# Reading both heads' scores out before the transposes, one copy moved to ScalarE, partial sums added later

## The chip, the cores and the metric

The kernel runs on one core of one Trainium2 chip. The metric is the time of one execution on the device, in microseconds (us); lower is better. The core has five engines with a queue each, which meet only through semaphores: TensorE (PE in the profile, its weight loads PEld), VectorE (DVE), ScalarE (ACT), GpSimd (POOL) and SyncE (SP, which here only issues DMAs). TensorE multiplies out of SBUF into PSUM, which has eight banks of 512 fp32 numbers in each of 128 partitions.

## The reference

Three parts follow one another: attention with a computed bias, a max-of-three layer, and an ELU layer.

```python
# q, k, v: 4 batches, 8 heads, 576 rows, 64 wide
scores = q @ k.T / sqrt(64) + bias          # bias from a small network of |i - j| and i
attn   = softmax(scores)                    # over 576 keys
x      = (attn @ v) as [2304, 512]
h      = max(x @ w1, x @ w2, x @ w3)        # 512 -> 768
x      = h @ w_out                          # 768 -> 512
out    = ELU(x @ w_in) @ w_out2             # 512 -> 2048 -> 512
```

All inputs are fp32, the weights of the later layers are given as 64-bit numbers that the kernel turns into fp32 itself.

## The kernel before

A first stage (to about 66 us) computes the bias and stores it to DRAM. The attention follows (to about 404 us), then the two layers, in which TensorE is busy nearly all of the time.

The attention works through 16 pairs of heads (n), and five blocks of query rows for each (c = 0 to 4): 80 steps, s = 5n + c. Blocks 0 to 3 are 128 rows of both heads; block 4 is the last 64 rows of both heads, packed into one tile of 128 partitions, so it has one read-out instead of two. I call five steps a group and name a step by the block whose scores it computes (step 0 to step 4).

What belongs to one block, in its order:
- `unit_qk` (L222, PE): scores of one head into one of two PSUM tiles, PB[0] and PB[1] (pb in the rows), two banks each.
- `scores` (L230, DVE): reads a head's scores out of PB, adds the bias and finds the row's extreme. I call the two of a step h0 and h1.
- `expo` (L235, ACT): the exponential, with its row sum.
- `recip` (L240, L241, DVE) and `diag` (L249, POOL): the reciprocal of the row sums, as a diagonal matrix.
- `trans` (L252, PE): turns the exponentials into the two PSUM tiles TQ (tq) and scales them with that diagonal, 32 products that the trace lists as 64 matmuls. The first 512 of the 576 keys fit there.
- `tails` (L252, PE): the last 64 keys of each head, turned into unused columns of PB[0], 4 products (8 matmuls). They lie in the same two banks as head 0's scores.
- `evac_tails` (L77, DVE) copies the tails out of PB[0]; `evac` (L75 on ACT or L77 on DVE) copies TQ[0] and TQ[1] out. EVD lists the blocks whose TQ[1] goes to DVE.
- `pv` (L319, L323, L327, PE): products with v into two PSUM tiles XO (xo), after the blocks 0 and 1, and after 2 to 4. When they are complete, `x_copy` (L341, ACT) takes XO[0], `x_sum` (L345, DVE) adds XO[1], `x_hi` and `x_lo` (POOL) split the sum into two parts for the next layer.
- `pump` (L420 to L430 and others): one piece of the decoding of a later layer's weights. Nearly all of them put one instruction on DVE, some one on ACT or POOL. One goes with each step past the sixth, except where c = 1.

The order is set by numbers. Every call is entered in a plan with a key, s plus an offset out of the table OFF; the plan is sorted by key and issued in that order, and each engine executes its own instructions strictly so. An offset above 1 or 2 means that the call is made one or two steps later: in step s, TensorE computes the scores of block s, turns the exponentials of block s - 2, and multiplies older blocks with v. Waits are derived from the order: a call that touches a PSUM bank which an earlier call of another engine touched waits for that call.

Of the kernel before, what the change touches and what calls it, by code (L numbers as in the profile page):

```python
# [31 lines left out]

OFF = {"qk0": 0.0, "qk1": 0.01, "t0": 0.30, "t1": 0.31, "pump": 0.32, "ns": 1.305, "dg": 1.306, "tr": 2.10, "tl": 2.20,
       "evt": 2.311, "ev0": 2.385, "ev1": 2.387, "ex0": 0.38, "ex1": 0.40}
PV_AT = {1: [(4.5, 0), (4.5, 1), (5.5, 2), (5.5, 3), (5.5, 4)],
         4: [(3.5, 0), (3.5, 1), (4.5, 2), (4.5, 3), (5.5, 4)]}
X_AT = {1: 5.6, 4: 5.6}
EVD = {0, 1, 2}  # L40

MOE_LD = 74.39
MOE_AT = [(79.60, 81.00), (80.60, 81.45), (82.00, None)]
# [10 lines left out]
def fused_kernel(ctx, tc, tkq, vv, lt, pk, wm1, wo1, win2, wo2, out):  # L54
# [16 lines left out]
    def hi_of(eng, dst, src):  # L71
        if eng == "p":
            nc.gpsimd.tensor_scalar(dst, src, 1.0, 1.0, op0=ALU.mult, op1=ALU.mult)
        elif eng == "a":
            nc.scalar.activation(dst, src, AF.Copy)  # L75
        else:
            nc.vector.tensor_copy(dst, src)  # L77
# [43 lines left out]
    with ExitStack() as pro:  # L121
# [18 lines left out]
        with tc.manual_schedule():  # L140
# [38 lines left out]
            for A in range(36):  # L179
# [15 lines left out]
                c, r = divmod(A, 8)  # L195
# [94 lines left out]
    def evac(s, g):  # L290
        n, c = steps[s]
        p = PT[n, c > 1][0]
        if c < 4:
            q0 = 128 * (c % 2) + 64 * g
            hi_of("v" if g and c in EVD else "a", p[:, :, q0:q0 + 64], TQ[g].rearrange("p (k q) -> p k q", k=8))
        else:
# [251 lines left out]
    def at(key, fn, *args):  # L548
        plan.append((key, len(plan), fn, args))

    for s, (n, c) in enumerate(steps):
        o = {nm: s + off for nm, off in OFF.items()}
        at(o["qk0"], unit_qk, s, 0)
        at(o["t0"], scores, s, 0)
        at(o["ex0"], expo, s, 0)
        if c < 4:
            at(o["qk1"], unit_qk, s, 1)
            at(o["t1"], scores, s, 1)
            at(o["ex1"], expo, s, 1)
        at(o["ns"], recip, s)  # L560
        at(o["dg"], diag, s)
        at(o["tr"], trans, s)
        at(o["tl"], tails, s)
        at(o["ev0"], evac, s, 0)
        at(o["ev1"], evac, s, 1)
        at(o["evt"], evac_tails, s)
        if c in (1, 4):
            for off, k in PV_AT[c]:
                at(s + off + 0.01 * k, pv, s, k)
            at(s + X_AT[c], x_copy, s)  # L570
            at(s + X_AT[c] + 0.25, x_sum, s)
            at(s + X_AT[c] + 0.5, x_hi, s)
            at(s + X_AT[c] + 0.75, x_lo, s)
        if s > 5 and c != 1:
            at(o["pump"], pump)
        if n % 4 == 3 and n < 15:
            at(s + 0.45, load_b, n // 4 + 1, c)
# [121 lines left out]
    def small(tag, bufs):  # L699
        return mp.tile([128, NB], F32, tag=tag, name=f"{tag}_t", bufs=bufs)  # L700
# [61 lines left out]
    with tc.manual_schedule():  # L762
        for n, u in enumerate(units + [None]):
# [6 lines left out]
            if n < 2:  # L770

                for i in range(2):
                    w = take_w(("wi", u[1], 3 * i))
                    v = take_w(("w3", pre[1], i)) if pre else None
                    for q, (b, d) in enumerate(((B11, B21), (B12, B22))):
# [3 lines left out]
                        c = small("c", 4)  # L779
# [121 lines left out]
```

## Time and profile before

| | |
|---|---|
| Runs | 1098.22, 1095.53, 1097.67 us; median 1097.67 |
| Profiled execution | 1097.02 us, of which the span of instructions is 1095.2 |
| PE | busy 989.3 us, 90% of the span |
| DVE | 708.7 us, 65% |
| ACT | 517.6 us, 47% |
| POOL | 339.3 us, 31% |
| Chain that ended last | PE 80%, DVE 16%, all others 4% |

The busy shares are means over stages with different limits. In the page's 40 slices PE is at 7 or 8 tenths in the attention and at 9 or more from the sixteenth slice on; DVE stands at 6 to 9 tenths in the attention. The 16% of the chain that run through DVE lie mostly in the attention.

### The profile page before, as it was taken

How to read it: one execution, taken by the hardware profiler on the slowest of the kernel's cores; microseconds unless marked ns; L12 is line 12 of the kernel's file. 1: busy time of each engine (PE TensorE's matmuls, PEld its weight loads, DVE VectorE, ACT ScalarE, POOL GpSimd, SP SyncE). 2: the span in 40 equal slices, each digit the busy share in tenths (PEclk: the TensorE clock that was granted, in tenths of full speed). 3: DMA queues.
4: the chain of work that ended last, by engine and by line, in shares of the span. 5: the costliest groups of instructions: out<-in, count | busy, mean ns of one | idle time of the engine just before them, and what ended most of it. 6: DMA issues, size and time to landing. Idle time of an engine off the chain costs nothing.

```text
span 1095.2 us, 28524 instructions
## 1 busy us (share of the span) xinstructions
PE 989.3 (90%) x11748; PEld 846.2 (77%) x11748; DVE 708.7 (65%) x1444; ACT 517.6 (47%) x1071; POOL 339.3 (31%) x419
## 2 busy tenths in 40 slices
PE   7967777777777679999999999999999999999998
PEld 3445555555455468999999999998999889988997
DVE  7946676667666665998878698174567436663333
ACT  8935555555555553333343334163445344444433
POOL 0002323223322233444345345122332323232212
PEclk9979999999999999999999999999999999999999
DMA  7731443343352213567798788325556655575553
GB/s 274 280 122 67 139 144 116 127 142 118 108 172 86 86 58 129 194 221 286 257 350 307 247 293 323 117 97 174 178 192 210 237 176 194 193 253 180 188 194 110
DMA packets 65905, 201.00 MB, mean 184 GB/s; under 512 B 7024, under 2 KB 14832, under 8 KB 65776
## 3 DMA queue, kind: packets, MB, share of 16 engines
q1 hardware_dynamic: 65776, 199.18, 53.0%
q8 instruction: 93, 1.52, 0.5%
q14 instruction: 36, 0.29, 0.1%
HBM read 150.78 MB, written 48.37 MB: 182 GB/s over the span
## 4 chain that ended last, share of the span: by engine, by line
PE 80%; DVE 16%; issue 2%; DMA 1%; ACT 0%; SPq 0%; POOL 0%; DVEq 0%; POOLq 0%; ACTq 0%
PE xo L696 16%; PE pb L740 12%; PE pb L526 11%; DVE e_t L230 9%; PE tq L252 7%; PE tq L740 6%; PE pb L222 5%; PE xo L526 5%; PE tq L526 5%; PE pb L620 3%; DVE p L77 3%; PE pb L183 2%; PE pbb L183 2%; PE xo L620 2%; PE tq L620 2%
## 5 line engine op out<-in xcount | busy, mean ns | idle before, releaser
L81 POOL TENSOR_TENSOR gl<-t_t,gh 128x384 fp32r<-128x384 f32 x96 | 108.8, 1144 | 286.0 <-ACT gh L75 286.0
L235 ACT ACTIVATE e_t<-e_t,st_t 128x576 f32<-128x576 f32 x144 | 111.1, 772 | 164.1 <-DVE st_t L240 155.2
L230 DVE CUSTOM_DVE_ANT_0 e_t<-pb,b_t 128x576 f32<-128x576 f32 x144 | 107.7, 748 | 88.3 <-PE pb L252 67.5
L222 PE MATMUL pb<-kq_t 64*64 64x288 f32 x1152 | 90.9, 425 | 74.0 <-DVE p L77 72.8
L249 POOL TENSOR_SCALAR dg_t<-ident,st_t 128x64 f32<-128x64 f32 x144 | 49.8, 359 | 264.3 <-DVE st_t L241 192.1
L222 PEld LDWEIGHTS pb<-kq_t 64*64 64x64 f32 x1152 | 36.5, 134 | 120.9 <-DVE p L77 105.8
L252 PEld LDWEIGHTS tq<-dg_t,e_t 64*64 64x64 f32 x4608 | 91.0, 139 | 41.0 <-DVE p L77 17.1
L740 PE MATMUL pb<-w_t,gh 128*128 128x512 f32 x384 | 119.3, 392 | 0.0
L526 PE MATMUL pb<-xh,w_t 128*128 128x384 f32 x448 | 116.9, 336 | 0.0
L252 PE MATMUL tq<-dg_t,e_t 64*64 64x64 f32 x4608 | 96.4, 225 | 18.5 <-DVE p L77 12.5
L696 PE MATMUL xo<-tt,w_t 128*128 128x384 f32 x528 | 107.4, 338 | 0.0
L696 PEld LDWEIGHTS xo<-tt,w_t 128*128 128x128 f32 x528 | 95.0, 188 | 7.5
L718 ACT ACTIVATE t_t<-c_t 128x384 f32<-128x384 f32 x96 | 50.0, 521 | 103.7 <-DVE c_t L709 95.5
L696 PE MATMUL xo<-xh,w_t 128*128 128x384 f32 x328 | 94.6, 335 | 0.0
L526 PEld LDWEIGHTS pb<-xh,w_t 128*128 128x128 f32 x448 | 81.2, 188 | 0.5 <-issue 0.4
L319 PE MATMUL xo<-p,tv_t 64*64 64x320 f32 (+1 forms) x1024 | 78.7, 408 | 0.9 <-issue 0.5
L740 PEld LDWEIGHTS pb<-w_t,gh 128*128 128x128 f32 x384 | 70.5, 188 | 6.6
L740 PE MATMUL pb<-w_t,gl 128*128 128x512 f32 x192 | 75.5, 393 | 0.0
L526 PE MATMUL pb<-xl,w_t 128*128 128x384 f32 x224 | 75.3, 336 | 0.0
L75 ACT ACTIVATE gh<-t_t 128x384 fp32r<-128x384 f32 x96 | 48.5, 519 | 33.4 <-DVE t_t L726 33.4
L696 PEld LDWEIGHTS xo<-xh,w_t 128*128 128x128 f32 x328 | 60.2, 188 | 3.0
L726 DVE SCALAR_TENSOR_TENSOR t_t<-t_t,c_t 128x384 f32<-128x384 f32 x96 | 59.0, 632 | 4.5 <-ACT t_t L719 4.1
(131 smaller groups left out, 2198.8 us busy)
## 6 DMA issues: line engine op xcount, KB each, us to landing
w_t<-scw_w SPq DMA_DIRECT2D x90, 512.0 KB, 4.4
w_t<-scw_wi SPq DMA_DIRECT2D x74, 512.0 KB, 3.6
kq_t<-tkq SPq DMA_DIRECT2D x16, 864.0 KB, 5.2
scw_wi<-sp SPq DMA_DIRECT2D x26, 512.0 KB, 4.7
scw_w<-sp SPq DMA_DIRECT2D x22, 512.0 KB, 5.3
raw<-wo SPq DMA_DIRECT2D x22, 512.0 KB, 3.8
scr<-o_t SPq DMA_DIRECT2D x36, 288.0 KB, 3.9
raw<-wm SPq DMA_DIRECT2D x18, 512.0 KB, 3.9
```

Source lines behind the costliest of these rows:

```text
L81: e.tensor_tensor(out=dst, in0=src, in1=hi.bitcast(F32), op=ALU.subtract)
L222: mm(PB[h][H64[g], 224 + 288 * r:512 + 288 * r], t[H64[r], 576 + 576 * a + q0:640 + 576 * a + q0], t[H64[r], 288 * a:288 * a + 288], start ...
L230: nc.vector.tensor_tensor_reduce(out=E[s][:, 576 * h:576 * h + 576], in0=PB[h][:, 224:800], in1=BT[n // 4, c, h], op0=ALU.add, op1=ALU.min ...
L235: nc.scalar.activation(e, e, AF.Exp, bias=st[:, h:h + 1], scale=-1.0, accum_out=st[:, 2 + h:3 + h])
L252: mm(dst, E[s][H64[g], k0:k0 + 64], DG[s][H64[g], h % nheads(s)], start=True, stop=True)
L319: mm(XO[g][H64[h], 0:w], v[H64[g], 128 * k + 64 * h:128 * k + 64 * h + 64], ps[0][H64[g], 4 * h + k, :], start=(k == 0), stop=(k == 3 and ...
L526: mm(ps[blk][:, 0:NB], wt[:, ks], xt[:, kk, t0:t0 + NB], start=(j == 0), stop=(j == 11))
L620: mm(ps[blk][:, 0:NB], WO[0][:, kk, wt, ms], xt[:, bs], start=(j == 0), stop=(j == 3 * NM1 - 1))
L696: mm(ps, w[wt][:, ks], b[xt][:, kk], start=(start and j == 0), stop=(stop and j == 5), skip_group_check=True)
L718: nc.scalar.activation(t, c, AF.Relu, scale=-1.0)
L726: pend.append([lambda: nc.vector.scalar_tensor_tensor(out=t, in0=t, scalar=-1.0, in1=c, op0=ALU.add, op1=ALU.max), last])
L740: mm(acc[t], g[:, ts], w[k], start=(f == 0 and i == 0 and j == 0), stop=(f == NU - 1 and i == 1 and j == 2))
```

## The change

Three entries of the tables and one offset change. `t0` and `t1` (h0 and h1) go from 0.30 and 0.31, behind `trans` and `tails`, to 0.02 and 0.03, ahead of them. `recip` and `diag` of the block before keep their place between the two read-outs. Block 1 leaves EVD, so the copy of its TQ[1] goes to ACT. `x_sum` goes from 0.25 to 0.427 behind `x_copy`, which is past the start of the next step, between `recip` and h1.

```diff
-OFF = {"qk0": 0.0, "qk1": 0.01, "t0": 0.30, "t1": 0.31, "pump": 0.32, "ns": 1.305, "dg": 1.306, "tr": 2.10, "tl": 2.20,
-       "evt": 2.311, "ev0": 2.385, "ev1": 2.387, "ex0": 0.38, "ex1": 0.40}
+OFF = {"qk0": 0.0, "qk1": 0.01, "t0": 0.02, "ns": 1.025, "dg": 1.026, "t1": 0.03, "tr": 2.10, "tl": 2.20, "evt": 2.311,
+       "pump": 0.32, "ev0": 2.385, "ev1": 2.387, "ex0": 0.38, "ex1": 0.40}
...
-EVD = {0, 1, 2}
+EVD = {0, 2}
...
-            at(s + X_AT[c] + 0.25, x_sum, s)
+            at(s + X_AT[c] + 0.427, x_sum, s)
```

On DVE, one whole step 3, before and then now; pb_99 is PB[0], pb_100 is PB[1], tq_860 is TQ[1], ISA is the read-out of scores or of its extreme, and the brackets name the engine whose semaphore is waited for.

```order
L230 ISA e_t,st_t<-pb_99,b_t 128x576 [waits PE_49]
L230 ISA st_t 128x1
L240 TENSOR_SCALAR st_t<-st_t 128x2 [waits Activation_49]
L241 RECIPROCAL st_t<-st_t 128x2 [waits DVE_49]
L230 ISA e_t,st_t<-pb_100,b_t 128x576
L230 ISA st_t 128x1
L77 COPY p_5274<-pb_99 128x128
L430 TENSOR_TENSOR t_w<-t_w,x_t 128x512
L77 COPY p_5273<-tq_860 128x8x64
```

```order
L230 ISA e_t,st_t<-pb_99,b_t 128x576 [waits PE_49]
L230 ISA st_t 128x1
L240 TENSOR_SCALAR st_t<-st_t 128x2 [waits Activation_49]
L241 RECIPROCAL st_t<-st_t 128x2 [waits DVE_49]
L230 ISA e_t,st_t<-pb_100,b_t 128x576 [waits PE_49]
L230 ISA st_t 128x1
L77 COPY p_5283<-pb_99 128x128 [waits PE_49]
L430 TENSOR_TENSOR t_w<-t_w,x_t 128x512
```

DVE's order is the same but for the copy of TQ[1], which is gone; but h1 and the copy of the tails, which before had nothing left to wait for once h0 had started, now have waits on PE of their own.

On PE, the end of the turning and the tails of one step, before and then now; xo_861 and xo_862 are XO[0] and XO[1].

```order
L252 MATMUL tq_859<-dg_t,e_t 64x64 x2
L252 MATMUL tq_860<-dg_t,e_t 64x64 x2
L252 MATMUL pb_99<-dg_t,e_t 64x64 x4
L319 MATMUL xo_861<-p_4252,tv_t 64x256 [waits DMAHW2_49,Activation_49]
L319 MATMUL xo_861<-p_4252,tv_t 64x256
L319 MATMUL xo_862<-p_4252,tv_t 64x256 [waits DVE_49]
```

```order
L252 MATMUL tq_859<-dg_t,e_t 64x64 x2
L252 MATMUL tq_860<-dg_t,e_t 64x64 x2
L252 MATMUL pb_99<-dg_t,e_t 64x64 [waits DVE_49]
L252 MATMUL pb_99<-dg_t,e_t 64x64 x3
L319 MATMUL xo_861<-p_4261,tv_t 64x256 [waits DMAHW2_49,Activation_49]
L319 MATMUL xo_861<-p_4261,tv_t 64x256
L319 MATMUL xo_862<-p_4261,tv_t 64x256 [waits DVE_49]
```

No matmul has moved; the first product of the tails has got a wait on DVE.

On DVE again, from the end of a step 4 into step 0, before and then now; L345 is `x_sum`.

```order
L77 COPY p_5410<-pb_99 128x128
L420 TENSOR_SCALAR x_t<-raw 128x512 [waits DMAHW4_49]
L77 COPY p_5409<-tq_860 128x8x64
L345 TENSOR_TENSOR xf<-xo_862,xf 128x320 [waits Activation_49]
L230 ISA e_t,st_t<-pb_99,b_t 128x576 [waits PE_49]
L230 ISA st_t 128x1
L240 TENSOR_SCALAR st_t<-st_t 128x1
L241 RECIPROCAL st_t<-st_t 128x1 [waits DVE_49]
L230 ISA e_t,st_t<-pb_100,b_t 128x576
```

```order
L77 COPY p_5418<-pb_99 128x128 [waits PE_49]
L420 TENSOR_SCALAR x_t<-raw 128x512 [waits DMAHW4_49]
L77 COPY p_5417<-tq_860 128x8x64
L230 ISA e_t,st_t<-pb_99,b_t 128x576 [waits PE_49]
L230 ISA st_t 128x1
L240 TENSOR_SCALAR st_t<-st_t 128x1 [waits Activation_49]
L241 RECIPROCAL st_t<-st_t 128x1 [waits DVE_49]
L345 TENSOR_TENSOR xf<-xo_862,xf 128x320 [waits Activation_49]
L230 ISA e_t,st_t<-pb_100,b_t 128x576 [waits PE_49]
```

`x_sum` has moved from ahead of h0 to between the reciprocal and h1.

## Rows read from the trace of the kernel before

**Rows 1.** Busy us by engine in two stretches, then clock, DMA share, GB/s.

```profile
66.00:78.00 12.00, 7.93 (x196) 6.03 (x188) 4.95 (x16) 4.21 (x10) 1.22 (x4) 0.50 0.07 10
90.00:400.00 310.00, 228.95 (x6724) 160.47 (x6720) 210.81 (x601) 169.04 (x407) 93.01 (x196) 0.99 0.35 118
```

**Rows 2.** Waits from 90 to 404 us: who for whom, us, times, longest.

```profile
ACT e_t L235 <- DVE st_t L240: 142.1, 72, 3.6
...
PE pb L222 <- DVE p L77: 65.5, 71, 1.1
DVE e_t L230 <- PE pb L252: 54.5, 58, 2.5
```

**Rows 3.** Chain of waits through a step 2 and beyond: start, us on it.

```profile
259.04 1.20 PE pb L222 x16
260.24 0.93 PE tq L252 x64
261.17 0.16 PE pb L252 x8
...
261.36 0.76 DVE e_t L230
...
262.40 0.65 DVE e_t L230
...
263.06 0.20 DVE p L77
263.27 1.14 DVE t_w L425
264.41 0.61 DVE p L77
```

**Rows 4.** Timeline of PE, starts of step 4, second and last group: start, us, instruction.

```profile
96.74 0.72 PE L222 MATMUL pb<-kq_t 64*64 64x288 f32 x8 [1.04 <-DVE p L77]
...
401.53 0.72 PE L222 MATMUL pb<-kq_t 64*64 64x288 f32 x8 [0.94 <-DVE p L77]
```

**Rows 5.** Timeline of PE: a step 4 begins, and a step 2.

```profile
268.35 0.72 PE L222 MATMUL pb<-kq_t 64*64 64x288 f32 x8 [0.94 <-DVE p L77]
268.88 0.29 PE L252 MATMUL tq<-dg_t,e_t 64*64 64x64 f32 x4
...
280.39 1.20 PE L222 MATMUL pb<-kq_t 64*64 64x288 f32 x16 [0.72 <-DVE p L77]
281.41 1.11 PE L252 MATMUL tq<-dg_t,e_t 64*64 64x64 f32 x64
282.34 0.30 PE L252 MATMUL pb<-dg_t,e_t 64*64 64x64 f32 x8
282.46 1.26 PE L319 MATMUL xo<-p,tv_t 64*64 64x320 f32 x16
```

**Rows 6.** Timeline of DVE in a step 1.

```profile
278.43 0.76 DVE L230 CUSTOM_DVE_ANT_0 e_t<-pb,b_t 128x576 f32<-128x576 f32 x1 [1.11 <-PE pb L252]
...
279.11 0.17 DVE L240 TENSOR_SCALAR st_t<-st_t 128x2 f32<-128x2 f32 x1
...
279.39 0.74 DVE L230 CUSTOM_DVE_ANT_0 e_t<-pb,b_t 128x576 f32<-128x576 f32 x1
...
280.06 0.28 DVE L77 COPY p<-pb 64x128 f32<-64x128 f32 x1
281.76 0.42 DVE L345 TENSOR_TENSOR xf<-xo,xf 128x256 f32<-128x256 f32 x1 [1.42 <-ACT xf L341]
```

**Rows 7.** Two decoding lines, 90 to 404 us: ns least/median/most.

```profile
L423 DVE TENSOR_SCALAR t_w<-raw x13: 410/1245/1517, 96.6 to 398.1; 128x512 int32<-128x512 int32 x13
...
L425 DVE SCALAR_TENSOR_TENSOR t_w<-raw,t_w x13: 680/691/1236, 100.2 to 401.4; 128x512 int32<-128x512 int32 x13
```

**Rows 8.** Timeline of ACT: two copies of TQ, then the second exponential.

```profile
276.30 1.07 ACT L75 ACTIVATE p<-tq 128x512 f32<-128x512 f32 x2
277.25 0.77 ACT L235 ACTIVATE e_t<-e_t,st_t 128x576 f32<-128x576 f32 x1
```

## The prediction

> **What bounds the kernel now.** I read the windows by stage first, then the waits, then the chain of waits through a few steps, and last the timelines of single engines for durations. In the attention from 90 to 400 us PE is busy 228.95 of 310 us and DVE 210.81, at a granted clock of 0.99 [rows 1]: neither is full, so the stage is bound by a hand-off between them. The waits say which. PE's scores wait 65.5 us in 71 waits for a copy by DVE, and DVE's read-out waits 54.5 us in 58 waits for L252 into pb, the tails [rows 2]. Each waits for the other once a step. The chain shows the circle [rows 3]: scores 1.20, turning 0.93, tails 0.16, then over to DVE with h0 0.76, h1 0.65, copy of the tails 0.20, and only then PE again; where a decoding instruction (1.14 there) and the copy of TQ[1] (0.61) follow on DVE, the next turning waits for these too. The reader is to see that h0 needs nothing but the scores, which had ended at 260.24, and starts at 261.36. That PE goes on to multiply with v meanwhile does not help the circle.
>
> A group takes 21.77 us: from step 4 at 96.74 to step 4 at 401.53 there are 14 groups in 304.79 us [rows 4].
>
> **What the change does to a step.** *h0 and h1 ahead of the turning.* h0 can start as soon as the eight matmuls of head 0 are through, about 0.75 us into a step (0.72 for these eight alone [rows 5], and 0.03 for the semaphore), and is read out beside the turning instead of after it. The circle is cut: the tails now wait for h0 (over for some time, as a rule), and the scores of the next step for the copy of the tails. What comes late next has to be found by laying the five steps out with the times of the trace, counted from start to start, as the engines overlap their instructions.
>
> PE [rows 5]: scores 1.02 (0.53 in step 4), turning 0.93, tails 0.12; block 4's turning half of that. Products with v by their columns from the scores (16 matmuls of 288 columns in 1.02): 0.91 for 256 columns, 1.13 for 320, 0.23 or 0.29 for the short ones. Step 0 adds up to 2.98, step 1 to 2.69, steps 2 and 3 to 3.20 each, step 4 to 1.87: 13.94 us a group. This is the floor.
> DVE [rows 6]: h0 0.68, reciprocals 0.28, h1 0.67, copy of the tails 0.28 to its end (0.20 to the next start), x_sum 0.42 or, by its columns, 0.52; copy of TQ[1] 0.61 [rows 3]. For a decoding instruction the two lines have medians of 0.69 and 1.25 [rows 7]; I take 0.85 at first, nearer to the first, since three of the five lines (L425, L427, L430) are of its kind, two inputs and one output.
> ACT [rows 8]: an exponential 0.77 from start to start, and two copies of TQ 0.95 together.
>
> Laid out, with step 1 starting at 0:
> - Step 1: h0 0.75 to 1.43, h1 done 2.38, copy of the tails done 2.66. PE is through at 2.76 and goes straight on.
> - Step 2: h0 3.51; x_sum now stands ahead of h1, which ends at 5.56; copy of the tails done about 5.8. PE through at 5.96, no loss. But the decoding runs to 6.6 and the copy of TQ[1] to 7.3.
> - Step 3: the turning, ready at 6.98, waits for that copy until 7.33 (0.35 lost). h0 starts at 7.21, still ahead of the tails. PE through at 9.51.
> - Step 4: short on PE. The tails wait for h0 until 11.07 (0.10 lost), the next scores for the copy of the tails until 11.77 (0.29 lost). Decoding and the copy of TQ[1] keep DVE until 13.1.
> - Step 0: the turning waits for TQ[1] until 13.22 (0.43 lost); h0 starts only at 13.1, then the reciprocal, x_sum and h1, so that the copy of the tails ends at 15.5 and step 1 begins at 15.55 (0.37 lost).
>
> So a group takes 15.55 us instead of 21.77. The DVE's queue is what is late next, in two places: behind the decoding in steps 2 and 4.
>
> *Block 1's TQ[1] on ACT.* It takes 0.61 from DVE in step 3 and puts 0.48 on ACT there, where ACT has room (its exponential of h1 ends about 10.7 and is next asked for at 10.94). Left on DVE it would hold h0 of step 4 and its turning, so I count it inside the layout.
>
> *x_sum later.* Behind it stand h1, the copy of the tails and so the next scores. In step 2 the cover is PE's 3.20 us; in step 0 it is part of the 0.37 lost. If it stayed where it was it would stand ahead of h0, which is no better. The products with v that overwrite XO[1] wait for it too, in step 0 by about 0.2 us, inside the loss named.
>
> *reciprocal and diag earlier in PE's time.* diag has a whole step until the turning asks for it. But the reciprocal now stands in DVE's queue behind h0 with a wait on ACT for the second exponential of the step before, and h1, the tails' copy and the next scores are behind it. By the layout that exponential is done 0.24 to 1.3 us earlier in each step, so I price it at nothing and keep it for a rival. No DMA moves on SP's queue and the bytes are the same; at a DMA share of 0.35 [rows 1] a third less time leaves it near 0.5, below a limit.
>
> *Decoding beside GpSimd.* L425 takes 0.68 at least and 1.24 at most [rows 7], with the same shape, so something beside it slows it. With the steps shorter, DVE and GpSimd lie beside each other more of the time. Bounds: nothing, or every decoding at 1.24, which in the two places where it decides adds 2 x 0.39 = 0.8 a group. I take 0.3, nearer to the median of 0.69: 15.85 us a group.
> The Trainium skill (SBUF — State Buffer, "Who interferes with whom") says that VectorE with two SBUF inputs and GpSimd share a port that whoever comes first locks for the whole instruction, the other being fully blocked. By that rule a decoding instruction could wait out a whole instruction of GpSimd; were that as long as the longest decoding, 1.24, the two places would cost 2.5 a group instead of 0.3, and the time would be 1040 us. The longest L425 in the trace is only 0.56 over the shortest, so the trace agrees that it is held up, but not for that long, and my bound stays by the rows.
>
> **The sum.** From step 4 of the first group to step 4 of the last there are 15 groups, and I use 21.77 for each: 15 x (21.77 - 15.85) = 88.8 us. The first steps, at half clock (0.50 from 66 to 78 us [rows 1]), lose the same idle time; 1 us for that. Nothing before them or after the last step changes; in the layers PE is the bound and the decoding is counted in steps, not in time, so it stands where it stood. 90 us off the profiled 1097.02 (span 1095.2 and 1.8 around it, 0.65 under the runs' median) gives **1007 us**.
>
> **Rivals.**
> *PE's floor.* If decoding mostly hits its short form (0.41 to 0.69) and the losses vanish, the group takes 13.94: 15 x 7.83 = 117 less, 980 us. Against it: DVE's own sum in the layout leaves it under a microsecond of idle time in step 4 to step 0. Between this and the forecast lies 980 to 995. Chance 0.10.
> *The hand-off through ACT.* The second exponential waits behind two copies of TQ on ACT, now also in step 3, and behind a weight instruction of ACT in some steps; where that makes it later by more than the 0.24 to 0.43 us that steps 4, 1 and 2 leave, DVE stands at the reciprocal, and h1, the tails' copy and PE with it. About 0.6 a group for that, 0.8 for decoding at its longest, and 0.3 for semaphores that I did not count give 17.25 a group: 15 x 4.52 + 1 = 69 less, 1028 us. For it: the waits of ACT for DVE now are 142.1 us [rows 2], so ACT is always just behind; against it, ACT is busy 169 of 310 us. 1022 to 1050. Chance 0.24.
> *Slower: PE's clock.* If the attention ran at 1.2 GHz, as from 66 to 78 us, PE's 13.94 would double and pass the old 21.77: the group would take some 29.5, which is 116 us more, 1213. It decides from the point where more than 5.9 / 13.94 = 42% of the stage runs at the low level. Against it: at a busy share of 74% the stage already has 0.99 [rows 1], and PE would idle less. Chance 0.03.
> *It does not do what it says.* If h0 went on waiting for the tails, only x_sum would be added to the circle (0.94 a group) and a copy taken from it (0.61): 5 us more, 1102. But the tails now wait for DVE, so such a wait would be a circle that never ends. Chance, with all other ways to no change, 0.02. Something between 1050 and 1094, by a wait I do not see: 0.03.
>
> **How the numbers follow.** The forecast's own case, 995 to 1022 us (15.1 to 16.9 a group), has 0.58. Range 985 to 1046: it takes in most of the ACT rival and of the way to the floor and leaves out about 0.15. About 0.3% (3.3 us) is what a measurement of this kernel can tell from no change: faster 0.95, within 0.02, slower 0.03.
>
> **What would show it.** The wait of DVE's L230 for L252 gone, h0 starting about 0.75 us after the scores or, in steps 3 and 0, straight behind the copy of TQ[1]; PE's waits for L77 at the scores small, with those left at steps 0 and 1 and at the turning of steps 3 and 0; the starts of step 4 at 15 to 17 us from one another; PE's busy share of the stage near 0.9 or more (about 14 of 15.85). A DVE that waits at L240 for ACT shows the second rival; a clock well under 0.99 the third. It is wrong if the groups keep more than 18 us, or if the layers after the attention become longer.

## The result, and the profile after

| | before | after |
|---|---|---|
| Median of the runs | 1097.16 us | 1010.32 us (1008.94 to 1012.75) |
| Ratio | | 0.9212, 95% interval 0.9191 to 0.9234 |
| Profiled execution | 1097.02, span 1095.2 | 1010.22, span 1008.4 |
| PE, DVE, ACT busy share of the span | 90, 65, 47% | 97, 69, 52% |
| Chain that ended last | PE 80%, DVE 16% | PE 91%, DVE 6% |

The change is faster by 7.9%, 3 us short of the 1007 us forecast. The time came from the attention. Its first and last step 4 stand at these places on PE now (start, duration, instruction; to hold against [rows 4]):

```profile
70.87 0.72 PE L222 MATMUL pb<-kq_t 64*64 64x288 f32 x8 [0.42 <-DVE p L77]
...
315.06 0.66 PE L222 MATMUL pb<-kq_t 64*64 64x288 f32 x8
```

Before, the first step 4 began so:

```profile
74.90 1.24 PE L222 MATMUL pb<-kq_t 64*64 64x288 f32 x8 [2.03 <-DVE p L77]
```

Now 15 groups lie between the first and the last in 244.19 us, 16.28 each. Before, it was from 74.90 to 401.53 [rows 4]: 326.63 us, 21.78 each. So 82.4 us come from the groups, 4.0 from what lies ahead of the first step 4, and 0.3 from what follows the last one (693.7 to the end of the span before, 693.3 now): 86.8 together.

The waits after, from 75 to 318 us, first PE's and then DVE's (who for whom, us in total, times, longest), answer to [rows 2]:

```profile
PE tq L252 <- issue: 5.3, 7, 1.7
PE tq L252 <- DVE p L77: 2.4, 4, 0.7
PE pb L252 <- issue: 1.7, 2, 1.2
PE pb L252 <- DVE st_t L230: 1.3, 5, 0.6
PE pb L222 <- issue: 1.3, 1, 1.3
PE xo L319 <- issue: 1.2, 2, 0.7
...
DVE e_t L230 <- PE pb L222: 30.5, 33, 2.3
DVE p L77 <- PE pb L252: 5.7, 18, 0.9
```

The two waits that made the circle are gone from their places: PE's scores no longer wait for the copy of the tails (65.5 us before, none listed now), and h0 waits for its scores, L222, instead of the tails. DVE never waits at L240 for ACT. What PE waits for now is a line that stood low before: "issue", 9.5 us in 12 places, time for which the trace knows no releaser.

The chain of waits through a step 4 and a step 0 (start, us on the chain) reads quite unlike [rows 3]:

```profile
203.95 0.43 PE pb L222 x7
204.38 0.98 PE tq L252 x63
205.37 0.30 PE pb L252 x8
205.66 0.43 PE xo L323 x4
206.10 0.09 PE xo L327 x2
206.19 1.09 PE pb L222 x16
207.28 0.93 PE tq L252 x64
208.21 0.12 PE pb L252 x8
```

It no longer crosses to DVE. DVE's timeline beside it shows the new order at work:

```profile
204.50 0.76 DVE L230 CUSTOM_DVE_ANT_0 e_t<-pb,b_t 128x576 f32<-128x576 f32 x1 [0.48 <-PE pb L222]
...
206.27 0.68 DVE L77 COPY p<-tq 128x512 f32<-128x512 f32 x1
206.88 0.75 DVE L230 CUSTOM_DVE_ANT_0 e_t<-pb,b_t 128x576 f32<-128x576 f32 x1
...
207.73 0.16 DVE L241 RECIPROCAL st_t<-st_t 128x1 f32<-128x1 f32 x1
207.81 0.47 DVE L345 TENSOR_TENSOR xf<-xo,xf 128x320 f32<-128x320 f32 x1
208.20 0.75 DVE L230 CUSTOM_DVE_ANT_0 e_t<-pb,b_t 128x576 f32<-128x576 f32 x1
208.87 0.28 DVE L77 COPY p<-pb 128x128 f32<-128x128 f32 x1
```

The first row is h0 of step 4: it waits for its scores, which PE began at 203.68, and for nothing else. In step 0, which PE began at 206.08, the copy of TQ[1], h0, reciprocal, x_sum, h1 and the copy of the tails follow without a gap and end at 209.15, just ahead of PE's next scores at 209.21. Here h0 starts at 206.88 because the copy of TQ[1] lets it, and runs beside PE's last scores and the turning, which begins at 207.10.

Busy time by stage after (window, its length, then busy us of PE, PEld, DVE, ACT and POOL, clock, DMA share, GB/s), for [rows 1]:

```profile
66.00:72.00 6.00, 5.17 (x144) 3.73 (x140) 3.26 (x10) 3.85 (x8) 0.60 (x2) 0.67 0.01 3
72.00:78.00 6.00, 4.92 (x170) 3.76 (x164) 3.42 (x13) 4.15 (x11) 0.92 (x3) 1.00 0.60 205
...
75.00:318.00 243.00, 228.99 (x7030) 191.22 (x7020) 201.53 (x613) 185.37 (x444) 98.56 (x204) 1.00 0.45 153
```

PE is busy 94% of the attention where it was 74%, DVE 83% where it was 68%. The stage is PE's now. And the clock is up earlier: it stood at 0.50 (1.2 GHz) from 66 to 78 us before, in which PE was busy 7.93 of 12 us [rows 1]; with PE busy 5.17 of 6 us from 66 to 72 it is mixed there and at its full 2.4 GHz after it. The eight matmuls of the first step 4 took 1.24 us before and 0.72 here.

### The profile page after: what moved, and what is told of

It is laid out like the page before. It is cut to its first block, busy times and chain, and to the rows that moved or that the text cites. A ratio compares the mean times of both kernels' runs of the same rounds, so it can differ in the third digit from the quotient of the medians.

```text
span 1008.4 us, 28525 instructions
## 1 busy us (share of the span) xinstructions
PE 977.4 (97%) x11748; PEld 869.2 (86%) x11748; DVE 692.1 (69%) x1428; ACT 526.1 (52%) x1087; POOL 341.7 (34%) x419
## 4 chain that ended last, share of the span: by engine, by line
PE 91%; DVE 6%; issue 1%; DMA 1%; ACT 0%; SPq 0%; POOL 0%; DVEq 0%; POOLq 0%; ACTq 0%
PE xo L696 18%; PE pb L740 13%; PE pb L526 12%; PE tq L740 6%; PE tq L252 6%; PE xo L319 6%; PE xo L526 5%; PE tq L526 5%; PE pb L222 5%; PE pb L620 4%; PE pb L183 3%; PE pbb L183 2%; DVE e_t L230 2%; PE xo L620 2%; PE tq L620 2%
## 5 line engine op out<-in xcount | busy, mean ns | idle before, releaser
L230 DVE CUSTOM_DVE_ANT_0 e_t<-pb,b_t 128x576 f32<-128x576 f32 x144 | 107.7, 749 | 32.7 <-PE pb L222 32.5
L252 PEld LDWEIGHTS tq<-dg_t,e_t 64*64 64x64 f32 x4608 | 96.6, 136 | 22.7 <-issue 7.7
L252 PE MATMUL tq<-dg_t,e_t 64*64 64x64 f32 x4608 | 97.8, 222 | 10.9 <-issue 5.3
L222 PE MATMUL pb<-kq_t 64*64 64x288 f32 x1152 | 98.6, 413 | 3.8 <-issue 1.3
L319 PE MATMUL xo<-p,tv_t 64*64 64x320 f32 (+1 forms) x1024 | 85.4, 408 | 1.6 <-issue 1.2
L75 ACT ACTIVATE p<-tq 128x512 f32<-128x512 f32 (+1 forms) x128 | 62.8, 528 | 16.4 <-PE tq L252 15.2
L222 PEld LDWEIGHTS pb<-kq_t 64*64 64x64 f32 x1152 | 50.9, 133 | 22.9 <-DVE p L77 4.4
```

The source lines that it names most:

```text
L222: mm(PB[h][H64[g], 224 + 288 * r:512 + 288 * r], t[H64[r], 576 + 576 * a + q0:640 + 576 * a + q0], t[H64[r], 288 * a:288 * a + 288], start ...
L230: nc.vector.tensor_tensor_reduce(out=E[s][:, 576 * h:576 * h + 576], in0=PB[h][:, 224:800], in1=BT[n // 4, c, h], op0=ALU.add, op1=ALU.min ...
L252: mm(dst, E[s][H64[g], k0:k0 + 64], DG[s][H64[g], h % nheads(s)], start=True, stop=True)
L319: mm(XO[g][H64[h], 0:w], v[H64[g], 128 * k + 64 * h:128 * k + 64 * h + 64], ps[0][H64[g], 4 * h + k, :], start=(k == 0), stop=(k == 3 and ...
```

## The experiments

Ratios are to the kernel before, run on the same chip in the same job; the medians of before differ by up to 3 us between jobs, so I compare ratios. "Group" is the mean over 15 groups from the first to the last reciprocal of a step 0 in the profiled execution, "issue" PE's idle time with that releaser between them (pieces above 0.15 us), and "rest" is the group without a fifteenth of it.

| run | ratio (95%) | group | issue (places) | rest |
|---|---|---|---|---|
| before | 1 | 21.63 | 3.9 (5) | 21.37 |
| the change | 0.9212 (0.9191 to 0.9234) | 16.25 | 9.5 (12) | 15.61 |
| order only | 0.9292 (0.9265 to 0.9320) | 16.96 | 12.0 (13) | 16.16 |
| only h0 moved | 0.9244 (0.9218 to 0.9270) | 16.49 | 9.1 (12) | 15.89 |
| x_sum early | 0.9226 (0.9199 to 0.9252) | 16.54 | 9.3 (10) | 15.92 |
| copy on DVE | 0.9252 (0.9235 to 0.9268) | 16.60 | 13.4 (14) | 15.71 |
| old order, copy on ACT | 0.9871 (0.9850 to 0.9891) | 21.00 | 2.3 (3) | 20.85 |
| all copies on ACT | 0.9208 (0.9171 to 0.9245) | 16.41 | 14.8 (13) | 15.42 |
| decoding after copies | 0.9196 (0.9172 to 0.9221) | 16.45 | 12.1 (17) | 15.64 |
| without later loads | 0.9096 (0.9077 to 0.9115) | 15.53 | 0 | 15.53 |
| load in four | 0.9204 (0.9182 to 0.9225) | 16.32 | 11.6 (14) | 15.55 |
| load in four, all copies on ACT | 0.9196 (0.9174 to 0.9218) | 15.97 | 11.0 (10) | 15.24 |
| the change again | 0.9199 (0.9181 to 0.9216) | 16.14 | 9.2 (8) | 15.53 |
| more traffic | 0.9564 (0.9544 to 0.9583) | 18.57 | 32.5 (28) | 16.41 |

**Order only.** The order of the change without its two small parts.

```diff
-EVD = {0, 2}
+EVD = {0, 1, 2}
...
-            at(s + X_AT[c] + 0.427, x_sum, s)
+            at(s + X_AT[c] + 0.25, x_sum, s)
```

> The change with its two smaller parts undone: block 1's TQ[1] is copied by DVE again and x_sum stands ahead of h0 again. My theory (the read-out of head 0 beside the turning is the gain, and what is left is DVE's queue): x_sum ahead of h0 waits in steps 1 and 2 for ScalarE's copy and makes a group about 0.6 us longer, the copy in step 3 holds the turning of step 4 and makes it 0.4 longer, together 15 x 1.0 = 15 us: 1025 us, so five sixths of the gain from the order alone. Rival, that the three parts only work together and the circle stays closed without them: above 1060 us. Rival, that the small parts are hidden: 1010 us.

Measured 0.9292, 1020 us: nine tenths of the gain (0.0708 of 0.0788) is the order. It is 9 to 10 us slower than the change, not 15; the rivals fall, the circle is open without the small parts, and these are not quite free.

**Only h0 moved.**

```diff
-OFF = {"qk0": 0.0, "qk1": 0.01, "t0": 0.02, "ns": 1.025, "dg": 1.026, "t1": 0.03, "tr": 2.10, "tl": 2.20, "evt": 2.311,
+OFF = {"qk0": 0.0, "qk1": 0.01, "t0": 0.02, "ns": 1.305, "dg": 1.306, "t1": 0.31, "tr": 2.10, "tl": 2.20, "evt": 2.311,
```

> The change, but only h0 is moved ahead of the turning; the reciprocal, the diagonal and h1 keep their old offsets. On DVE that swaps only x_sum and the reciprocal. My theory: only h0 shares PSUM banks with the tails, so this is all that the circle needs, and the time is that of the change within 3 us (1008 to 1013 us). Rival, that reading out both heads early is what gains (the words of the change): half of the gain or more is lost, above 1050 us.

Measured 0.9244. So 96% of the gain is there with h0 alone moved (the two small parts kept): it was the read-out that shares banks with the tails, and not "both heads" that closed the circle. The 3 to 5 us that are missing touch the noise (the intervals overlap with the change's first one, not with its second); in the trace PE waits 6.0 us for the copy of TQ[1] where it waited 2.4. Why, I did not settle.

**x_sum early.**

```diff
-            at(s + X_AT[c] + 0.427, x_sum, s)
+            at(s + X_AT[c] + 0.25, x_sum, s)
```

> The change with x_sum back at 0.25 behind x_copy, so ahead of h0 on DVE. The prediction called that place no better than the new one. Laid out anew: in step 2 x_sum waits for ScalarE's copy until about 4.2 us where h0 could start at 3.5, and h0, h1 and the copy of the tails come about 0.9 us later, 0.6 of it past PE's cover: 15 x 0.6 = 9 us, 1019 us. If the prediction's sentence holds: 1010 us within 3.

Measured 0.9226, 1.5 to 3 us over the change and inside the noise. The wait that I expected is there, in DVE's waits of this run:

```profile
DVE xf L345 <- ACT xf L341: 20.6, 17, 1.6
DVE e_t L230 <- PE pb L222: 14.6, 27, 2.0
```

DVE stands 20.6 us at x_sum for ACT, which it never did in the change, but it takes most of it from time in which it would have waited for scores (30.5 us there, 14.6 here). A new wait, paid for out of an old one.

**Copy on DVE.**

```diff
-EVD = {0, 2}
+EVD = {0, 1, 2}
```

> The change with block 1's TQ[1] copied by DVE again. My theory: in step 3 it stands behind the decoding on DVE and ends about 10.5 us into the group, 0.5 after the turning of step 4 is ready for it; about 0.4 a group comes through: 1016 us, with PE's L252 into tq waiting for DVE's L77 in step 4. Rival, that PE has cover for it: 1010 us within 3.

Measured 0.9252, 1015.7 us where 1016 was expected. PE's turning waits 4.4 us in 11 places for DVE's copies (2.4 in 4 in the change), but issue is also 4 us more in this execution. The direction is right, though the interval is only just clear of the change's first one. The rest of the group is 0.10 to 0.18 us longer than in the two runs of the change, 1.5 to 2.7 us in 15 groups: of the 6 us expected, less than half is shown to be the copy.

**The old order with the copy on ACT.**

```diff
-EVD = {0, 1, 2}
+EVD = {0, 2}
```

> The kernel before with one part of the change: block 1's TQ[1] copied by ScalarE. My theory: in the old order the turning of step 4 waited about 0.4 to 0.7 us for that copy behind the decoding; 15 x 0.4 = 6 us less, 1091 us. Rival, that the copy only gains in the new order: 1097 us within 3.

Measured 0.9871, twice what I expected: the copy is worth 14 us in the old order by the ratio (9.5 by the two profiled spans, 1095.2 and 1085.7). In its trace PE's waits for the copies of TQ fall from 12.5 to 6.7 us, which is the 6 us that I had worked out; that the whole group becomes 0.6 us shorter, I can't assign further.

**All copies on ACT.**

```diff
-EVD = {0, 2}
+EVD = set()
```

> The change with every copy of TQ on ScalarE, so DVE has none in steps 2 and 4 either. My theory (DVE's queue behind the decoding in steps 2 and 4 is what is late): the turning of steps 3 and 0 no longer waits for DVE, h0 of these steps starts 0.5 us earlier, and the group loses about 0.5: 15 x 0.5 = 8 us less, 1002 us. Rival (the hand-off through ACT): two more copies stand ahead of the second exponential, DVE waits at L240 for ACT, and the time is 1015 us or more.

Measured 0.9208, like the change. DVE still does not wait at L240 for ACT, so the hand-off rival falls even with two more copies ahead of the second exponential. PE no longer waits for DVE's copies, and the rest of the group falls by 0.1 to 0.2 us against the two runs of the change; but the profiled execution has 14.8 us of issue, one piece of it 5.0 us long, and the runs spread from 1005.93 to 1015.58. This sent me to the issue line.

**Decoding after the copies.**

```diff
-       "pump": 0.32, "ev0": 2.385, "ev1": 2.387, "ex0": 0.38, "ex1": 0.40}
+       "pump": 0.39, "ev0": 2.385, "ev1": 2.387, "ex0": 0.38, "ex1": 0.40}
```

> The change with the decoding issued behind the copies of TQ instead of ahead of them (0.39 for 0.32). My theory: TQ[1] is free about 0.85 us earlier in steps 2 and 4, so that the turning of steps 3 and 0 does not wait for it, but h0 of these steps is as late as before since DVE does the same work: 0.35 of the group's losses goes, 5 us less, 1005 us. Rival, that what is left is not DVE's queue but PE's own stalls (the idle time that the trace puts down to issue): 1010 us within 3.

Measured 0.9196, no difference. The rest of the group is 15.64 us, as in the change. PE's waits for the copies of TQ are gone, but they were only 2.4 us in all, not the 0.35 a group that I had; and PE's waits for h0 rose from 1.3 to 3.5 us. The little that there was to gain moved from one wait to another.

**Without the later loads.**

```diff
     def load_kq(n):
+        if n > 1:
+            KQ[n] = KQ[n - 2]
+            return
...
     def load_v(n):
+        if n > 1:
+            TV[n] = TV[n - 2]
+            return
...
     def load_b(hp, c):
+        if hp:
+            for h in range(2 if c < 4 else 1):
+                BT[hp, c, h] = BT[0, c, h]
+            return
```

> The change without the loads of q, k, v and bias after the first: later groups use the tiles of the first two head pairs and the bias of the first pair of heads, so the output is not the reference's. PE's work is the same; of the attention's DMA traffic about two thirds goes. The question is PE's idle time put down to issue, 9.5 us in 12 places of the attention, each 2 to 3 us behind a packet of the instruction queue. If bulk transfers delay the fetch of PE's instructions: less than 3 us of it is left and the attention is 5 to 7 us shorter. If the fetch takes that long by itself: 8 to 11 us in about 12 places, as now, and the time stays within 3 us of 1010.

Measured 0.9096, 11 to 13 us below the change. Issue is not less, it is zero: no piece above 0.15 us is left. The attention in this run and the waits of PE in it (75 to 318 us; L262 and L240 are L252 and L230 of the other kernels):

```profile
75.00:307.00 232.00, 226.65 (x7041) 189.08 (x7034) 199.45 (x613) 183.44 (x443) 100.22 (x204) 1.00 0.15 54
```

```profile
PE pb L262 <- DVE st_t L240: 2.9, 13, 0.6
PE tq L262 <- DVE p L77: 2.0, 3, 0.7
PE xo L329 <- DVE p L77: 0.3, 1, 0.3
```

At 54 GB/s instead of 153 PE is busy 97.7% of the stage, and a group takes 15.53 us.

**Load in four, alone and with all copies on ACT.**

```diff
-        at(5 * n + 0.2, load_kq, n + 1)
+        for i in range(4):
+            at(5 * n + i + 0.2, load_kq_part, n + 1, i)
```

where the new call loads 432 of the 1728 columns; the second kernel has `EVD = set()` besides.

> The change with the load of q and k of the next head pair cut into four, one piece in each of four steps, same bytes. The run without loads had no idle time of PE put down to issue and was 11 us shorter. If it is the backlog of a single long transfer (864 KB, about 5 us) that holds the fetch of PE's instructions: issue falls from some 10 us to 5 or less, and the time is 4 to 6 us under the change on the same chip. If it is the traffic as such: issue stays at 8 to 13 us and the time is the same within 3 us.

> The load in four, and all copies of TQ on ScalarE. With issue taken out, the run with all copies on ScalarE had 15.43 us a group where the change has 15.61, so this part is worth 15 x 0.2 = 3 us. If cutting the load helps: 7 to 9 us under the change on the same chip; if not: 0 to 3 us.

Measured 0.9204 and 0.9196, beside 0.9199 for the change on the same chip: nothing. Issue stays at 11 to 12 us with the load in pieces. So it is not the backlog of this one transfer; other loads, of up to 512 KB, stayed whole. Of the kernels that keep every load the second one has the best group, 15.97, but its time can't be told from the change's. I have no version that beats the change.

**The change again.** No edit.

> The change itself, unaltered, as the measure for the others of this job: 1008 to 1013 us; issue anywhere from 8 to 14 us, as the variants showed.

Measured 0.9199, 1009.3 us, issue 9.2 us in 8 places.

**More traffic.**

```diff
+    def load_again(n):
+        t = kq.tile([128, 864], F32, tag="kq2", name="kq2_t", bufs=1)
+        nc.sync.dma_start(t, tkq[n][:, 0:864])
...
         at(5 * n + 0.2, load_kq, n + 1)
+        for i in range(1, 5):
+            at(5 * n + i + 0.2, load_again, n)
```

> The change with four more loads of 432 KB in each group, half of q and k again, into a tile that nothing reads: 1.7 MB a group more on top of about 2.4. If traffic delays the fetch of PE's instructions: issue rises to 20 us or more and the time to 1018 us or more. If the link with traffic is chance: issue 8 to 14 us, time within 3 us of the change.

Measured 0.9564: 1050 us, 40 us more than the change, with no work added to any engine but DMA issues. PE's waits in it from 75 to 340 us, and the stage (L256 is L252):

```profile
PE tq L256 <- issue: 18.0, 17, 2.5
PE pb L256 <- issue: 8.0, 6, 2.8
PE xo L323 <- issue: 3.1, 2, 2.7
PE pb L226 <- issue: 2.0, 2, 1.3
PE xo L327 <- issue: 1.4, 1, 1.4
```

```profile
75.00:318.00 243.00, 209.86 (x6373) 175.82 (x6367) 177.40 (x553) 168.18 (x400) 86.44 (x184) 0.99 0.70 234
```

Issue is 32.5 us at 234 GB/s, 23 us more than in the change. But not all of the 40 us is traffic. All the added loads share one buffer, so each waits in SP's queue until the last has landed, and what stands behind them in that queue is issued late. In SP's waits from 75 to 340 us, and then on DVE:

```profile
SPq L100 <- DMA kq_t<-tkq: 173.7, 53, 9.3
```

```profile
340.41 0.43 DVE L424 TENSOR_SCALAR x_t<-raw 128x512 int32<-128x512 int32 x1 [8.62 <-DMA raw<-wo]
```

L100 is the added load. A load of weights for the decoding (raw) went out only at 336.00; DVE stood 8.6 us at the decoding for it, the next h0 behind that, and PE 9.0 us for h0, in the one group that took 27.1 us. This part comes from how the experiment was built, and not from what traffic does to PE.

## Why the prediction was right

**The circle, and how it opens: right.** The cause (h0 waiting for tails that share its banks) was shown by the experiment that moves h0 alone. Where h0 waits for nothing but its scores, it starts later in the step than the 0.75 us forecast, but not by much: at 204.50 in the step 4 that PE began at 203.68, 0.82 us (also the median of all steps 4), and a median of 1.05 us in steps 2. Before, it was 2.51 and 2.32.

**The sum: right for a mix of reasons.** I laid out 15.55 us a group without contention; the run in which nothing but the fetch of data was taken out has 15.53. That these agree is luck: the two terms in it were each off by 1.2, against each other:

- *PE's floor*, 13.94, was too low. In the run without later loads a group nearly without delay looks like this on PE (starts, from a step 1 to the next step 0):

```profile
106.71 1.20 PE L232 MATMUL pb<-kq_t 64*64 64x288 f32 x16
...
109.70 0.46 PE L232 MATMUL pb<-kq_t 64*64 64x288 f32 x2
...
113.06 1.38 PE L232 MATMUL pb<-kq_t 64*64 64x288 f32 x16
...
116.32 0.76 PE L232 MATMUL pb<-kq_t 64*64 64x288 f32 x8
116.81 1.20 PE L262 MATMUL tq<-dg_t,e_t 64*64 64x64 f32 x64
117.96 0.34 PE L262 MATMUL pb<-dg_t,e_t 64*64 64x64 f32 x8
118.12 0.38 PE L333 MATMUL xo<-p,tv_t 64*64 64x256 f32 x1
...
118.72 1.20 PE L232 MATMUL pb<-kq_t 64*64 64x288 f32 x16
```

  Steps 1 to 4 take 2.99, 3.36, 3.26 and 2.40 us; with the 3.13 of a step 0 in the change (206.08 to 209.21) that is 15.14. The term that was mis-sized is "products with v by their columns", and with it the turning: step 4 was forecast at 1.87, but its turning takes 1.15 where 0.93 was taken from a step 2, and its short products 0.60 where columns gave 0.29; the products of step 0 take 1.06 (208.15 to 209.21) and not 0.91; step 1's 2.69 is 2.99, 0.18 of it a wait. Why the turning is slower in step 4 stays open. No group of any run is under 14.96, so the rival "PE's floor, 980 us" rested on a floor that does not exist.
- *DVE's lateness*, 1.6 a group (0.35, 0.10, 0.29, 0.43, 0.37 and 0.07), was too high: 15.53 less 15.14 leaves 0.4, and PE's waits for DVE in that run, 5.2 us in all, come to 0.3 a group. That DVE catches up because step 4 is longer on PE, and because the decoding is often in its short form, is likely and not shown.

The total came out 3 us over the forecast by errors that cancel: the groups gave 82.4 us where 88.8 were forecast, what lies ahead of them 4.0 where 1 was, and what follows them 0.3 where nothing was.

**Decoding beside GpSimd: wrong.** I added 0.3 a group. After the change the median of L425 is 0.681 and its longest 1.268 (0.691 and 1.236 before, [rows 7]). Of the 62 decoding instructions of L420 to L430 on DVE, from 90 to 407 us before and from 80 to 320 us after, 28 took more than 0.9 us before and 20 after, and the mean went from 0.88 to 0.81: the overlap became less, not more. The Trainium skill (SBUF — State Buffer, "Who interferes with whom") says that a VectorE instruction with two SBUF inputs and a GpSimd one that reads SBUF contend for a shared port. No run here contradicts it, but counting on more of it because the steps are shorter was an error.

**Issue: not seen.** In the place of that 0.3 stand 0.64 us a group of PE's idle time that I did not forecast, although the trace of before had 3.9 us of it. 15.53 + 0.64 gives 16.2, the 16.14 to 16.28 measured. That it hangs on traffic is shown: 0, 9.5, and 32.5 us at 54, 153 and 234 GB/s (9.1 to 14.8 in the new-order variants with the loads of the change).

What is starved is the fetch of PE's instructions, and the traces show it twice. In all twelve places of the change one packet of the queue that the profile's page calls "instruction" (q8) starts between 3 and 2 us ahead of the end of the stall, and none in the last 2 us; there are 56 such packets from 75 to 318 us. And if all of PE's records are counted from the start of a run (weight loads, matmuls, and 337 waits and drains, 23833 in the change), each of the 159 places of the table, over all runs, has 193 or 194 records more than a multiple of 256 ahead of it: these stalls come where one packet's instructions end and the next one's begin, and nowhere else. The Trainium skill (Runtime: NRT & Kernel Launch, "Instruction fetch mechanics") says that an engine's sequencer fetches its instructions by a DMA queue of its own in blocks of 256, and that this is mostly hidden. The profile agrees on the size: 93 packets for PE's 11748 matmuls and as many weight loads are 253 a packet, 256 with the waits and drains. It is hidden in one stage here and not in the other. In the layers of the change, from 330 to 1000 us, a block takes 23.8 us (median) at 213 GB/s, PE is busy 669.4 of 670 us and no place of issue is left; in the attention, at 153 GB/s, a block takes 4.4 us (mean), and the fetch is not always hidden.

Beside more data, the packet starts later. From the first instruction of a block on PE to the start of the packet that brings the next block, the median is 0.74 us in the run without later loads, 1.17 in the change and 1.53 with more traffic; in the change alone it is 0.96 in the 23 places where the 3 us before the packet moved less than 100 GB/s, and 2.25 in the 18 with more than 250. PE goes on 2.2 to 2.7 us after the packet's start in each of the twelve stalls. So blocks come late beside data; which part of the way the two share stays open, as no run changed the fetch alone.

**First steps: too small.** I gave them 1 us; they gave 4.0. Two waits of PE's scores for the copy of the tails, at the first step 4 and the step before it, were 2.03 us each and are 0.42 and 0.41 now: 3.2 us, the same circle with everything on PE at half clock. The first turning starts 0.46 us earlier (64.06 for 64.52), and about 0.3 us is the clock, which rose within these steps now and after them before.

**The rivals.** ACT's hand-off did not decide: DVE does not wait at L240 in the change, nor with all copies on ACT; with the decoding behind the copies it waits there 0.7 us in 3 places. The clock did the opposite of the slower rival. That x_sum's old place is "no better" can't be told from the times; its wait for ACT there, 20.6 us, shows that the old place needs cover.

## What to carry to other kernels

When two engines each wait for the other once a step and neither is full, look for the read that waits for more than it reads: here a read-out stood behind a later product that only shared its PSUM banks, and issuing it ahead of that product gave nine tenths of the gain. To size such a gain, take the busy engine's durations from the very step that they belong to, not scaled from another one. And when an engine comes to run short instructions without pause (256 in 4.4 us here), its own fetch of instructions becomes a cost that grows with the DMA traffic beside it; with long ones (256 in 23.8 us) it did not.

## What I had not expected of the hardware

PE's unexplained stalls sit only where a new block of 256 instructions begins, and depend on the data that moves beside them: none at 54 GB/s, 9.5 us of a stage of 244 us at 153, 32.5 at 234, single stalls of up to 5 us. They also make much of the spread between the groups of one execution: those of the change lie between 15.15 and 17.74 us, with 0 to 2.1 us of issue in each. Cutting the longest transfer into four changed nothing.
